# Order of one attention slot: scores and attention times v ahead of the second mixing, and the high copy between score copy and exponential

## Chip, cores and metric

The kernel runs on 1 core of one Trainium2 chip. The metric is the device time of one execution in microseconds (us), the median of several runs. Each run of the kernel before is listed below.

## What is computed

A talking-heads attention (4 batches, 12 heads, 448 tokens, 64 per head) is followed by two feed-forward blocks of 1792 tokens. The change lies in the attention alone. `w_pre` and `w_post` are 12 x 12 matrices that mix the heads before and after the softmax.

```python
scores = scale * np.matmul(q, k.transpose(0, 1, 3, 2))
scores = np.einsum('bhij,hg->bgij', scores, w_pre)      # first mixing
scores = scores - np.max(scores, axis=-1, keepdims=True)
attn = np.exp(scores)
attn = attn / (np.sum(attn, axis=-1, keepdims=True) + 1e-09)
attn = np.einsum('bhij,hg->bgij', attn, w_post)         # second mixing
return np.matmul(attn, v).astype(np.float32)            # a times v
...
a = x @ w1
b = x @ w2
h = a * b @ w3
x = h @ w_out
...
h = x @ w_in
r = np.maximum(h, 0.0)
return ((r * r) @ w_out).astype(np.float32)
```

## The kernel before

**Tiles.** The queries of each batch are cut into four groups of 110, 110, 110 and 118 rows, 16 groups `s` in all. For each group the scores of all 12 heads are made on TensorE in six pairs of heads (`qk`, L241, six matmuls each), copied from PSUM by ScalarE (`evict_s`, L248, the score copy) into one tile `S`. A DMA (`regroup`) then gathers 10 queries x 12 heads = 120 rows of 448 scores into a block `Bt`. There are 180 blocks `u`, 11 or 12 for each group. Everything that follows is done block by block:

- `premix` (L284, TensorE, float32, four matmul records for two blocks): the first mixing, into one of three PSUM banks `p`.
- `negmax` (L298, VectorE): the negative maximum of each row.
- `expo` (L306, ScalarE): the exponential with the row sum. It is the last reader of the bank `p`; its release comes with a second record, ACTIVATION_READ_ACCUMULATOR.
- `norm` (L322, L336, VectorE, for two blocks at once): the inverse of the sum.
- `split_h` (L353 on GpSimd, in some blocks L351 on ScalarE) and `split_l` (L367 on VectorE for even blocks, L364 and L365 on GpSimd for odd ones): the scaled exponential as two float16 halves `EH` and `EL`.
- `postmix` (L380, TensorE): the second mixing, 12 matmuls of 120 columns, into one of two PSUM banks `o`; the attention comes out transposed.
- `at_h` (L396, ScalarE): the high half of that result in float16, the high copy; `at_l` (L402, VectorE): the low half, which needs the high one and frees the bank `o`.
- `av` (L494, TensorE): attention times v for two heads of a whole group, in two parts of 12 matmuls each, once all blocks of the group have been through `at_l`. The result is copied by `put_xh` (L513, ScalarE) and `put_xl` (L522, VectorE) for every third pair of heads.

**Slots.** A loop over `u` from 0 (line 1332) writes the order of every engine's queue out by hand (`tc.manual_schedule()`, line 624), so the order in the program is the order on each engine. Slot `u` does the maximum and the exponential of block `u`, the halves of blocks `u-2` and `u-3`, `postmix(u-4)`, `at_h(u-5)` and `at_l(u-5)`. An odd slot does the first mixings of two blocks, `u+1` and `u+2`; an even slot none.

**Events.** Work for whole groups is put on slots ahead of the loop (lines 549 to 620): a list of `(kind, number, function, arguments)` for each slot, where `kind` is one of LOAD, FIRST, MID, LOW and END, and `do(kind)` carries out those of one kind. `qk` and `av` are END, with `store_x` and two steps of the scale of v; `evict_s` is FIRST of the next slot (MID in two crowded slots), `put_xh` FIRST and `put_xl` MID of the slot behind the third and sixth `av`. The splits of q, k and v are MID and LOW. Six slots of each group of 11 or 12 carry one `qk`, and most of these one `av` too.

**The order in a slot** is, in short: LOAD; `at_h`; two `premix` (odd slots); `negmax`; FIRST; `expo`; `norm`, `split_h`, `split_l`; `postmix`; `at_l`; MID; LOW; END; `regroup`. `AHEAD` is (5, 7): in these two slots `postmix` comes ahead of `premix`. `NB` is 180, `LAG` is 4 and `LEAD` is 5.

Of the kernel before, what the change touches and what calls it, by code (L numbers as in the profile page):

```python
# [24 lines left out]
LAG = 4  # L25
# [9 lines left out]
def talking_heads_attention_moe_moe2(  # L35
# [55 lines left out]
    def psum(pool, tag, dt=F32):  # L91
        return pool.tile([P, 512], dt, tag=tag, name=tag)
# [171 lines left out]
    NB = len(BLK)  # L264
# [16 lines left out]
    def premix(u):  # L281
        n = BLK[u][2]
        pt = psum(ps_p, "p")
        nc.tensor.matmul(  # L284
            pt[: n * H, :S],
            wpre_k.rearrange("p t g -> p (t g)")[: n * H, : n * H],
            Bt.pop(u)[: n * H],
            start=True,
            stop=True,
        )  # L290
        Pp[u] = pt

    def negmax(u):

        n, j = BLK[u][2] * H, u % 2
        if j == 0:
            nsum[u] = nsum[u + 1] = bp.tile([NBK, 6, 2], F32, tag="st", name="st", bufs=3)
        nc.vector.tensor_reduce(  # L298
            nsum[u][:n, 0, j : j + 1], Pp[u][:n, :S], axis=AX.X, op=ALU.max, negate=True
        )  # L300

    def expo(u):
        n, j = BLK[u][2] * H, u % 2
        t = nsum[u]
        e = bp.tile([NBK, EG, EW], F32, tag="E", name="E", bufs=4)[:, :, : S // EG]
        nc.scalar.activation(  # L306
            e[:n],
            Pp.pop(u)[:n, :S].rearrange("p (a b) -> p a b", a=EG),
            AF.Exp,
            bias=t[:n, 0, j : j + 1],  # L310
            scale=1.0,
            accum_out=t[:n, 1, j : j + 1],
        )
        Ex[u] = e

    def norm(u):

        t = nsum[u]
        rows = [BLK[x][2] * H for x in (u, u + 1)]
        if rows[0] == rows[1]:  # L320
            n = rows[0]
            nc.vector.tensor_scalar(  # L322
                t[:n, 2:5, :],
                t[:n, 1, :].unsqueeze(1).to_broadcast([n, 3, 2]),
                1e-9, 2.0 ** -11, op0=ALU.add, op1=ALU.mult,
            )
        else:
            for a in (0, 1):
                n = rows[a]
                nc.vector.tensor_scalar(  # L330
                    t[:n, 2, a : a + 1], t[:n, 1, a : a + 1], 1e-9, 2.0 ** -11,
                    op0=ALU.add, op1=ALU.mult,
                )
        for a in [slice(0, 2)] if rows[0] == rows[1] else [slice(0, 1), slice(1, 2)]:
            n = rows[a.start]
            nc.vector.reciprocal(t[:n, 5, a], t[:n, 2, a])  # L336
# [7 lines left out]
    def low_on_pool(u):  # L344
        return u % 2 == 1

    def split_h(u):
        n = BLK[u][2] * H
        EH[u] = bp.tile([NBK, S], F16, tag="EH", name="EH", bufs=4)
        if low_on_pool(u) and (u in full or u >= LAST_EH):  # L350
            nc.scalar.activation(seven(EH[u][:n]), Ex[u][:n], AF.Copy, scale=inverse(u))  # L351
            return
        nc.gpsimd.tensor_scalar(  # L353
            seven(EH[u][:n]), Ex[u][:n], inverse(u), 1.0, op0=ALU.mult, op1=ALU.mult
        )

    def split_l(u):
        n = BLK[u][2] * H
        e = Ex.pop(u)[:n]
        EL[u] = bp.tile([NBK, S], F16, tag="EL", name="EL", bufs=4)  # L360
        a, b = (seven(x[:n]) for x in (EL[u], EH[u]))
        if low_on_pool(u):
            f = bp.tile([NBK, EG, EW], F32, tag="F", name="F", bufs=1)[:n, :, : S // EG]
            nc.gpsimd.tensor_scalar(f, e, inverse(u), 1.0, op0=ALU.mult, op1=ALU.mult)  # L364
            nc.gpsimd.tensor_tensor(a, f, b, op=ALU.subtract)  # L365
        else:
            nc.vector.scalar_tensor_tensor(  # L367
                a, e, inverse(u), b, op0=ALU.mult, op1=ALU.subtract
            )

    def postmix(u):
        s, m, nr = BLK[u]
        n = nr * H
        pt = psum(ps_o, "o")
        hh, ll = EH.pop(u), EL.pop(u)
        wh = wpost_h[nr].rearrange("p g t -> p (g t)")
        wl = wpost_l[nr].rearrange("p g t -> p (g t)")
        for c in range(NCH):
            for i, (a, w) in enumerate(((hh, wh), (hh, wl), (ll, wh))):
                nc.tensor.matmul(  # L380
                    pt[:CP, c * n : (c + 1) * n],
                    a[:n, c * CP : (c + 1) * CP],
                    w[:n, :n],
                    start=(i == 0),
                    stop=(i == 2),
                )
        Po[u] = pt

    def at_h(u):
        s, m, nr = BLK[u]  # L390
        if m == 0:
            ATs[s] = tuple(
                bp.tile([CP, NCH, H, RMAX], F16, tag=f"AT{x}", name=f"AT{x}") for x in "hl"
            )
        src = Po[u][:CP, : NCH * nr * H].rearrange("p (c g t) -> p c g t", c=NCH, g=H)
        nc.scalar.copy(ATs[s][0][:, :, :, m * NR : m * NR + nr], src)  # L396

    def at_l(u):
        s, m, nr = BLK[u]
        src = Po.pop(u)[:CP, : NCH * nr * H].rearrange("p (c g t) -> p c g t", c=NCH, g=H)  # L400
        a = slice(m * NR, m * NR + nr)
        nc.vector.tensor_tensor(  # L402
            ATs[s][1][:, :, :, a], src, ATs[s][0][:, :, :, a], op=ALU.subtract
        )
# [127 lines left out]
    def load_x(z, b, i, k):  # L532
        if (b, i) == (0, 0):
            xall.append(sp.tile([P, NDC, NT], F16, tag="S", name="x"))
        n = S if b < B - 1 else sum(ROWS[:-2])
        cs = slice(i * NDC // k, (i + 1) * NDC // k)
        nc.sync.dma_start(xall[z][:, cs, b * S : b * S + n], x_d[z, b, :, cs, :n])
# [9 lines left out]
    LOAD, FIRST, MID, LOW, END = range(5)  # L547
# [85 lines left out]
    def keep_busy(n):  # L633
        for _ in range(n):
            nc.tensor.matmul(idle, zeros[:, :P], zeros, start=True, stop=True)
# [58 lines left out]
    AHEAD = (5, 7)  # L694
# [450 lines left out]
    def load_to(n):  # L1145
        while done[0] < min(n, limit[0]):
            load_w(done[0])
            done[0] += 1
# [180 lines left out]

    mlp_start = first[NSUP - 1] - 4  # L1330
    early = iter(())
    for u in range(NB + LAG + 2):
        if u == NB - LEAD:
            limit[0] = len(chunks)
            load_to(2 + LOADS)
        if u == mlp_start:
            kst.close()
            pools["w"] = ctx.enter_context(tc.tile_pool(name="wp", bufs=2, side="right"))
        if u in W_LOADS:
            load_to(W_LOADS.index(u) + 1)  # L1340
        if u == c0:
            early = (x for x in pair_steps(0, None) if x[2])
        if u == NB - LEAD + 1:
            for b in range(B):
                load_x(1, b, 0, 1)
        work = sorted(events.pop(u, []), key=lambda e: e[0])

        def do(now):
            for kind, _, f, a in work:
                if kind == now:  # L1350
                    f(*a)

        do(LOAD)
        if 0 <= u - LAG - 1 < NB - LAG:
            at_h(u - LAG - 1)
        if u in AHEAD:
            postmix(u - LAG)
        if u % 2:
            for x in (u + 1, u + 2):
                if x < NB:  # L1360
                    premix(x)
        if u in FILL:
            keep_busy(FILL[u])
        if u < NB:
            negmax(u)
        do(FIRST)
        if u < NB:
            expo(u)
        if u % 2 == 0 and 0 <= u - 2 < NB:
            norm(u - 2)  # L1370
        if 0 <= u - 2 < NB:
            split_h(u - 2)
            if low_on_pool(u - 2):
                split_l(u - 2)
        if 0 <= u - 3 < NB and not low_on_pool(u - 3):
            split_l(u - 3)
        if 0 <= u - LAG < NB and u not in AHEAD:
            postmix(u - LAG)
        if 0 <= u - LAG - 1 < NB - LAG:
            at_l(u - LAG - 1)  # L1380
        do(MID)
        do(LOW)
        for eng, cost, f in islice(early, STEPS.get(u, 0)):
            f()
        do(END)
        if NB <= u < NB + LAG:
            assert next(early, None) is None
            allow[0] = place["w1", 2]
            at_h(u - LAG)
            at_l(u - LAG)  # L1390
            first_tile(u - NB)
        if u + LEAD < NB:
            regroup(u + LEAD)
        if u - mlp_start in X_HIGH:
            load_x(0, *divmod(X_HIGH.index(u - mlp_start), 2), 2)
# [923 lines left out]
```

## Time and profile before

| | |
|---|---|
| runs of the kernel before | 1226.0, 1224.4, 1220.56 us (median 1224.4) |
| profiled execution | 1220.15 us, span of its trace 1218.4 us |
| TensorE matmuls busy | 1206.0 us (99% of the span) |
| TensorE weight loads | 746.8 us (61%) |
| VectorE (DVE) | 946.1 us (78%) |
| ScalarE (ACT) | 804.5 us (66%) |
| GpSimd (POOL) | 587.9 us (48%) |
| chain that ended last | TensorE 88%, VectorE 7%, ScalarE 2% |

The profile is one execution, read on the core's engines. PE is TensorE's matmuls, PEld its weight loads, DVE VectorE, ACT ScalarE, POOL GpSimd. Attention takes the first 440 us or so of the span. The matmul records overlap, since TensorE is a pipeline and the end of a matmul is modelled: a second mixing's matmuls are shown as 0.22 us each and start 0.05 us apart. So the busy share of TensorE says little about short stalls, and the starts say more. In the timeline consecutive instructions of one line and shape stand in one row with their count. A row ends with the idle time in front of it and what released it, where there was any.

### The profile page before, as it was taken

How to read it: one execution, taken by the hardware profiler on the slowest of the kernel's cores; microseconds unless marked ns; L12 is line 12 of the kernel's file. 1: busy time of each engine (PE TensorE's matmuls, PEld its weight loads, DVE VectorE, ACT ScalarE, POOL GpSimd, SP SyncE). 2: the span in 40 equal slices, each digit the busy share in tenths (PEclk: the TensorE clock that was granted, in tenths of full speed). 3: DMA queues.
4: the chain of work that ended last, by engine and by line, in shares of the span. 5: the costliest groups of instructions: out<-in, count | busy, mean ns of one | idle time of the engine just before them, and what ended most of it. 6: DMA issues, size and time to landing. Idle time of an engine off the chain costs nothing.

```text
span 1218.4 us, 26225 instructions
## 1 busy us (share of the span) xinstructions
PE 1206.0 (99%) x9904; PEld 746.8 (61%) x9904; DVE 946.1 (78%) x1690; ACT 804.5 (66%) x1620; POOL 587.9 (48%) x569
## 2 busy tenths in 40 slices
PE   7999999999999999999999999999999999999998
PEld 4666777676676765555558975555555555666665
DVE  6988899888889956766676875798778775999773
ACT  6888888878888735554454555568879776654430
POOL 4898788889879610101001311446143424666340
PEclk9999999999999999999999999999999999999999
DMA  6466555655645853655533537354478659656562
GB/s 196 128 160 166 136 146 135 170 126 152 177 115 163 240 131 101 161 135 158 138 131 127 190 120 245 110 168 167 162 259 280 236 192 325 196 159 184 175 193 79
DMA packets 139907, 205.02 MB, mean 168 GB/s; under 512 B 33828, under 2 KB 114852, under 8 KB 139780
## 3 DMA queue, kind: packets, MB, share of 16 engines
q1 hardware_dynamic: 139220, 202.41, 56.3%
q8 instruction: 78, 1.28, 0.5%
q0 software_dynamic: 560, 0.93, 0.4%
q14 instruction: 49, 0.40, 0.1%
HBM read 114.60 MB, written 50.16 MB: 135 GB/s over the span
## 4 chain that ended last, share of the span: by engine, by line
PE 88%; DVE 7%; ACT 2%; DMA 1%; issue 1%; SPq 0%; POOL 0%; ACTq 0%; DVEq 0%; POOLq 0%
PE mm L1259 25%; PE mm L1873 16%; PE mm L2125 16%; PE p L284 8%; PE o L380 7%; PE mm L1537 5%; PE s L241 4%; PE a L494 4%; DVE ATl L402 2%; DVE st L298 2%; DVE EL L367 2%; PE p L1259 1%; ACT E L306 1%; ACT ATh L396 0%; DMA Bt<-S 0%
## 5 line engine op out<-in xcount | busy, mean ns | idle before, releaser
L1259 PE MATMUL mm<-x,w 128*128 128x448 f16 x1044 | 197.7, 352 | 0.0
L1259 PEld LDWEIGHTS <-w 128*128 128x128 f16 x1134 | 110.5, 98 | 102.8
L1873 PE MATMUL mm<-x,wq 128*128 128x448 f16 x882 | 169.3, 352 | 0.0
L284 PE MATMUL p<-Bt,wpre_k 120*120 120x448 f32 x360 | 159.2, 560 | 3.1 <-DMA Bt<-S 2.6
L2125 PEld LDWEIGHTS <-ao 128*128 128x128 f16 x1176 | 115.0, 98 | 76.0
L380 PEld LDWEIGHTS <-EH 120*112 120x112 f16 (+1 forms) x1440 | 124.6, 130 | 44.7 <-issue 36.5
L1873 PEld LDWEIGHTS <-wq 128*128 128x128 f16 x882 | 86.0, 98 | 79.8 <-issue 0.3
L402 DVE TENSOR_TENSOR ATl<-o,ATh 112x480 f16<-112x480 f32 x180 | 116.1, 645 | 24.2 <-ACT ATh L396 23.7
L353 POOL TENSOR_SCALAR EH<-E,st 120x448 f16<-120x448 f32 (+1 forms) x152 | 112.6, 749 | 46.0 <-DVE st L336 34.6
L306 ACT ACTIVATE E<-p,st 120x448 f32<-120x448 f32 x180 | 116.3, 646 | 23.9 <-DVE st L298 14.6
L396 ACT CAST ATh<-o 112x480 f16<-112x480 f32 x180 | 101.1, 562 | 39.8 <-PE o L380 34.8
L380 PE MATMUL o<-wph,EH 120*112 120x120 f16 x720 | 124.0, 219 | 1.4 <-DVE ATl L402 1.1
L380 PE MATMUL o<-wph,EL 120*112 120x120 f16 x720 | 122.0, 216 | 0.0
L380 PE MATMUL o<-wpl,EH 120*112 120x120 f16 x720 | 122.0, 216 | 0.0
L365 POOL TENSOR_TENSOR EL<-F,EH 120x448 f16<-120x448 f32 (+1 forms) x90 | 104.0, 1155 | 31.7 <-issue 18.5
L298 DVE TENSOR_REDUCE st<-p 120x1 f32<-120x448 f32 x180 | 110.2, 613 | 1.2 <-PE p L284 0.7
L1259 PE MATMUL mm<-h,M 128*128 128x448 f16 x576 | 110.2, 353 | 0.0
L2125 PE MATMUL mm<-x,ao 128*128 128x384 f16 x588 | 96.5, 326 | 0.0
L2125 PE MATMUL mm<-ow,ao 128*128 128x384 f16 x588 | 96.0, 326 | 0.0
L380 PEld LDWEIGHTS <-EL 120*112 120x112 f16 x720 | 93.6, 130 | 0.0
L367 DVE SCALAR_TENSOR_TENSOR EL<-E,st,EH 120x448 f16<-120x448 f32 (+1 forms) x90 | 82.9, 921 | 11.1 <-POOL EH L353 10.6
L1259 PEld LDWEIGHTS <-M 128*128 128x128 f16 x576 | 55.9, 98 | 52.0 <-DVE M L1447 0.8
(266 smaller groups left out, 2535.8 us busy)
## 6 DMA issues: line engine op xcount, KB each, us to landing
Bt<-S SPq DMA_DIRECT2D x176, 210.0 KB
raw<-in_moe_w_out_dram SPq DMA_DIRECT2D x24, 768.0 KB
g<-ev SPq DMA_DIRECT2D x64, 224.0 KB
gt<-g SPq DMA_DIRECT2D x56, 256.0 KB
raw<-in_moe_w_in_dram SPq DMA_DIRECT2D x16, 768.0 KB
raw<-in_moe_w_dram SPq DMA_DIRECT2D x14, 768.0 KB
raw<-in_moe_w_dram SPq DMA_DIRECT2D x16, 512.0 KB
kept_out<-xa SPq DMA_DIRECT2D x16, 384.0 KB
```

Source lines behind the costliest of these rows:

```text
L284: nc.tensor.matmul(pt[: n * H, :S], wpre_k.rearrange("p t g -> p (t g)")[: n * H, : n * H], Bt.pop(u)[: n * H], start=True, stop=True,)
L298: nc.vector.tensor_reduce(nsum[u][:n, 0, j : j + 1], Pp[u][:n, :S], axis=AX.X, op=ALU.max, negate=True)
L306: nc.scalar.activation(e[:n], Pp.pop(u)[:n, :S].rearrange("p (a b) -> p a b", a=EG), AF.Exp, bias=t[:n, 0, j : j + 1], scale=1.0, accum_ou ...
L353: nc.gpsimd.tensor_scalar(seven(EH[u][:n]), Ex[u][:n], inverse(u), 1.0, op0=ALU.mult, op1=ALU.mult)
L365: nc.gpsimd.tensor_tensor(a, f, b, op=ALU.subtract)
L367: nc.vector.scalar_tensor_tensor(a, e, inverse(u), b, op0=ALU.mult, op1=ALU.subtract)
L380: nc.tensor.matmul(pt[:CP, c * n : (c + 1) * n], a[:n, c * CP : (c + 1) * CP], w[:n, :n], start=(i == 0), stop=(i == 2),)
L396: nc.scalar.copy(ATs[s][0][:, :, :, m * NR : m * NR + nr], src)
L402: nc.vector.tensor_tensor(ATs[s][1][:, :, :, a], src, ATs[s][0][:, :, :, a], op=ALU.subtract)
L1259: nc.tensor.matmul(pt[:, :S], w[a][:, cs], x[z][:, sl], start=(c == 0 and i == 0), stop=(c == len(parts) - 1 and i == 2),)
L1873: nc.tensor.matmul(pt[:, :S], w[:, a, c * P : (c + 1) * P], xop(t, b, kb, c), start=(start and c == 0 and m == 0), stop=(c == 2 and m == 2 ...
L2125: nc.tensor.matmul(pt[:, :OH], y[:, a, q * P : (q + 1) * P], ow[g, q][kb][:, w], start=(start and q == 0 and m == 0), stop=(q == NQ - 1 an ...
```

## The change

The loop of the slots is edited in five places. A slot behind number 7 that carries a `qk` or an `av` is called a `visit`. In a visit `postmix(u-4)` is issued behind END, so behind the scores and a times v of the slot, instead of ahead of `at_l`. In the slot behind a visit (`behind`) `at_h(u-5)` is issued behind FIRST, so behind the score copy and `put_xh`, and ahead of `expo(u)`; before, it was the first of the slot. Nothing is computed differently, and no instruction is added or removed.

```diff
@@ -1329,6 +1329,7 @@
     early = iter(())
+    behind = False
     for u in range(NB + LAG + 2):
@@ -1351,7 +1352,8 @@
         do(LOAD)
-        if 0 <= u - LAG - 1 < NB - LAG:
+        visit = max(AHEAD) < u < NB and any(e[0] == END and e[2] in (qk, av) for e in work)
+        if 0 <= u - LAG - 1 < NB - LAG and not behind:
             at_h(u - LAG - 1)
@@ -1364,6 +1366,8 @@
         do(FIRST)
+        if behind:
+            at_h(u - LAG - 1)
         if u < NB:
             expo(u)
@@ -1374,7 +1378,7 @@
-        if 0 <= u - LAG < NB and u not in AHEAD:
+        if 0 <= u - LAG < NB and u not in AHEAD and not visit:
             postmix(u - LAG)
@@ -1383,6 +1387,9 @@
         do(END)
+        if visit:
+            postmix(u - LAG)
+        behind = visit and u + 1 < NB
         if NB <= u < NB + LAG:
```

## Rows read from the trace of the kernel before

**Rows 1.** Windows: busy us and count by engine, 40 to 395 us, then clock, DMA
```profile
40.00:395.00 355.00, 353.89 (x4577) 247.41 (x4576) 310.09 (x670) 295.56 (x656) 302.66 (x333) 1.00 0.57 148
```

**Rows 2.** Waits of weight loads, same stretch: total us, times, longest us
```profile
PEld p L284 <- ACT E L306: 13.3, 35, 0.8
```

**Rows 3.** Timeline of TensorE, beat of slots 45 and 46: start, us, what
```profile
116.62 1.76 PE L284 MATMUL p<-Bt,wpre_k 120*120 120x448 f32 x4
...
118.22 0.22 PE L380 MATMUL o<-wph,EH 120*112 120x120 f16 x1
...
121.06 1.39 PE L284 MATMUL p<-Bt,wpre_k 120*120 120x448 f32 x3
```

**Rows 4.** Timeline of TensorE, beat of slots 91 and 92
```profile
222.12 1.72 PE L284 MATMUL p<-Bt,wpre_k 120*120 120x448 f32 x4
222.92 0.54 PE L284 MATMUL p<-Bt,wpre_k 120*120 120x448 f32 x1
223.67 0.22 PE L380 MATMUL o<-wph,EH 120*112 120x120 f16 x1
...
224.25 0.22 PE L380 MATMUL o<-wph,EL 120*112 120x120 f16 x1
224.40 0.46 PE L241 MATMUL s<-kh,qh 64*110 64x448 f32 x2
224.69 0.36 PE L241 MATMUL s<-kl,qh 64*110 64x448 f32 x2
224.89 0.37 PE L241 MATMUL s<-kh,ql 64*110 64x448 f32 x2
225.19 0.24 PE L494 MATMUL a<-ATh,Vh 112*64 112x110 f16 x2
...
225.90 0.26 PE L380 MATMUL o<-wph,EH 120*112 120x120 f16 x1
...
226.52 0.22 PE L380 MATMUL o<-wph,EL 120*112 120x120 f16 x1
226.57 1.34 PE L284 MATMUL p<-Bt,wpre_k 120*120 120x448 f32 x3
```

**Rows 5.** Timeline of TensorE: second mixings of even event slots behind a stall
```profile
49.79 0.21 PE L380 MATMUL o<-wph,EH 120*112 120x120 f16 x1
...
184.08 0.21 PE L380 MATMUL o<-wph,EH 120*112 120x120 f16 x1 [0.47 <-DVE ATl L402]
...
383.43 0.21 PE L380 MATMUL o<-wph,EH 120*112 120x120 f16 x1 [0.36 <-DVE ATl L402]
```

**Rows 6.** Timeline of ScalarE, the beat of rows 4
```profile
222.32 0.56 ACT L396 CAST ATh<-o 112x480 f16<-112x480 f32 x1
222.78 0.64 ACT L306 ACTIVATE E<-p,st 120x448 f32<-120x448 f32 x1
...
224.50 0.57 ACT L396 CAST ATh<-o 112x480 f16<-112x480 f32 x1 [0.39 <-PE o L380]
225.30 0.91 ACT L248 COPY S<-s 110x896 f32<-110x896 f32 x1 [0.23 <-PE s L241]
226.10 0.64 ACT L306 ACTIVATE E<-p,st 120x448 f32<-120x448 f32 x1
226.63 0.20 ACT L306 ACTIVATION_READ_ACCUMULATOR E<-p,st 120x1 f32 x1
```

**Rows 7.** Timeline: first mixings of odd beats that waited for an exponential
```profile
92.24 1.94 PE L284 MATMUL p<-Bt,wpre_k 120*120 120x448 f32 x4
...
101.38 2.03 PE L284 MATMUL p<-Bt,wpre_k 120*120 120x448 f32 x4
102.12 0.21 ACT L306 ACTIVATION_READ_ACCUMULATOR E<-p,st 120x1 f32 x1
102.39 0.64 PE L284 MATMUL p<-Bt,wpre_k 120*120 120x448 f32 x1
...
365.29 1.98 PE L284 MATMUL p<-Bt,wpre_k 120*120 120x448 f32 x4
```

## Prediction, made before the changed kernel was run

> **What bounds the kernel now.** I read the busy table of the attention stretch first, since the change touches nothing behind it [rows 1]. From 40 to 395 us TensorE is busy for 353.89 of 355 us; VectorE, ScalarE and GpSimd have 13 to 17% free, and the granted clock is 1.00. So TensorE's work sets the pace, and another order of its instructions can win only what TensorE waits, or the turn-round between kinds of matmul. Next I read the waits of TensorE's weight loads [rows 2]: 13.3 us in 35 places for the exponential (L306), which frees the bank that a first mixing (L284) writes. Much of that is a loader waiting beside a running matmul; so I then read the timeline from start to start, where a true stall shows as a longer step.
>
> Two slots make one beat: two first mixings (L284), two second mixings (L380), and in nearly every beat one set of scores (L241) and a times v (av, L494). The 94 slots that the change treats ("event slots", counted from lines 549 to 620) are 44 even and 50 odd ones. In a beat whose event slot is even, TensorE's order is first, first, second, second, scores, av [rows 3]; where it is odd: first, first, second, scores, av, second [rows 4]. Both beats take the same time: 121.06 - 116.62 = 4.44 us and 226.57 - 222.12 = 4.45 us.
>
> **Direct work on TensorE.** Nothing is added or removed; 12 matmuls of a second mixing move behind the scores and av.
> - Even beats become first, first, second, scores, av, second: the order of today's odd beat. Step by step: the first mixings take 118.22 - 116.62 = 1.60 us behind av [rows 3] and 223.67 - 222.12 = 1.55 us behind a second mixing; in exchange the second mixing that comes behind av lengthens from 224.25 - 223.67 = 0.58 to 226.52 - 225.90 = 0.62 us [rows 4]. Sum: 0.0, as the two beat lengths say.
> - Odd beats become first, first, scores, av, second, second. One neighbour is new: scores straight behind a first mixing. Bounds from the turns of today: from a first to a second mixing nothing is lost (from the later first mixing at 222.92 to 223.67 are 0.75 us, two passes of 0.38); from a second mixing into the scores 224.40 - 224.25 = 0.15, where matmuls of a mixing stand 0.05 apart, so 0.10 is lost; from scores into av 225.19 - 224.89 = 0.30 against 224.89 - 224.69 = 0.20 inside the scores, 0.10 again [rows 4]. So the old turn's 0.10 goes and the new one costs 0 to 0.10: a gain of 0 to 0.10 a beat, 0 to 5 us over 50. I take 0: the two turns that lose time are those where the tile shape changes (120x112, 64x110, 112x64), behind a step of 0.05 and one of 0.20 alike, and the new turn changes it too. The Trainium skill (TensorEngine Tiling (Array Packing), Key Properties) says that a change of tiling mode drains TensorE; the two turns agree, and no row shows the new one. By that rule this part is 0 us, without it -5 us.
>
> **Stalls that go.** In an even beat the later second mixing stands 0.58 us behind the earlier one, and it takes the bank of the one two before it, which the low part (L402) must have read. In five places it stalls, read as the step less 0.05: 0.24 (at 49.79, the first), 0.63, 0.16, 0.04 and 0.52 us (at 383.43, the last), 1.6 us in all; the two large ones show as idle time even by the modelled ends [rows 5]. All five are in even event slots, where this mixing now starts later by scores and av, 225.90 - 224.25 = 1.65 us [rows 4], more than any stall. Gain: 1.6 us. Next late behind the bank would be the half EL, and it wins the same 1.65 us.
>
> **What comes later.** ScalarE's high copy (L396) needs the second mixing; in odd beats that now ends later. And the change puts the copy behind the score copy (L248, 0.91 us) and, every third event, the copy of av's result (L513). Queued behind the high copy on ScalarE is the exponential of the same slot; behind that waits the second first-mixing of the next beat, for its bank (there are three). Today, in the beat of [rows 4, 6]: high copy 224.50, score copy 225.30, exponential 226.10 to 226.83. The mixing that waits is due 222.92 - 222.12 = 0.80 us into the next beat, at 226.57 + 0.80 = 227.37: 0.54 us of slack.
>
> After: the scores start 0.63 us earlier (0.58 and a step of 0.05), so the score copy starts at 225.30 - 0.63 = 224.67 and hands over 0.80 later (226.10 - 225.30), at 225.47. The moved mixing issues its last matmul at 226.52 - 0.58 - 0.05 = 225.89; high copy 0.25 later (224.50 - 224.25), at 226.14. So the copy placed in front costs nothing here: the wait for the second mixing hides it, with 0.67 us to spare (some 0.3 with L513); without that cover it would cost its 0.80. Exponential 0.46 after the copy (222.78 - 222.32), at 226.60; released after 0.73 (226.83 - 226.10), at 227.33; the mixing goes 0.06 after a release (102.39 - 102.33 [rows 7]), at 227.39. It is due at 227.37: a tie.
>
> So the slack of 0.54 is used up in odd beats: 4.45 us by TensorE's work, 4.47 by the loop through second mixing, high copy, exponential, first mixing, scores and av. What a lost race costs is seen where it is lost today: the two mixings at 101.38 last 2.03 us against 1.72 [rows 4, 7], +0.31, of which 0.10 is a weight load that wasn't done ahead (0.64 against 0.54). There are six such places, the first at 92.24 and the last at 365.29, of 0.18 to 0.31 us, 1.5 us in all; I count half as gone, since the score copy in front of the exponential no longer waits behind the high copy there. Of the 50 odd event slots 9 have another one right behind, whose scores and av give the loop over 1.6 us more; 41 remain. Bounds for each: 0 (in time) and 0.2 (tie lost by 0.1, 0.1 of weight load). I take 0.05, near the computed 0.02: 2.0 us. In about ten of them ScalarE has more to do (L433, L351 or L466 beside L513), so that its copy is late by itself: 0.1 more each, 1.0 us.
>
> On VectorE the low part (L402) waits for the high copy, and behind it are queued the splits, the next maximum (L298) and EL. VectorE has 44.9 of 355 us free [rows 1], 0.56 us a beat, and the maximum behind the low part is wanted by ScalarE only after one more high copy. Cost 0; where splits fill the gap, up to 0.3 a beat. In even beats the exponential comes no later, for the same two copies were ahead of it before. SP's DMA issues and GpSimd's work keep their order; nothing is moved past them. The last 35 us of attention have shorter beats and more av: +-0.5.
>
> **Sum.** -1.6 - 0.7 + 2.0 + 1.0 = +0.7 us. The profiled execution took 1220.15 us (span 1218.4), 4.25 below the median of 1224.4, at the lower end of the three runs (1220.56 to 1226.0). So 1221 for a profile like that one, and 1225.0 for the median.
>
> **The rivals.**
> - The tie is lost everywhere (slower). In odd beats the loop through the exponential takes TensorE's place as the bound. Place: the second first-mixing of each beat; it decides at a release later than 0.06 us before the mixing is due. Price: 41 x 0.2 = 8.2, less 1.6: 1231. For it: the slack computes to -0.02, and ScalarE has extra work in some beats. Against it: today's six losses add up to 1.5 us only. Chance 0.13.
> - The new turn is free (faster): scores behind a first mixing load their weights under its 0.38 us pass. 50 x 0.10 + 1.6 = 6.6: 1218. Against it: the turn behind the scores' 0.20 us pass hides nothing [rows 4]. Chance 0.06.
> - That the order isn't what the change says is no rival: the kernel writes it out by hand.
>
> **How the numbers follow.** Forecast 1225.0, chance 0.81, with its bounds (from -1.6 - 1.5 to about +6) 1221 to 1231. With the scatter of a median and the faster rival's end the range is 1218 to 1232. A measurement of this kernel can tell about 0.5%, 6.1 us: faster than 1218.3 has 0.06, slower than 1230.5 has 0.13, the rest 0.81.
>
> **What would show it.** Right: beats of 4.44 to 4.50 us of either kind; no stall on L402 at a second mixing of an even event slot; ScalarE's wait for the high copy's mixing now behind the score copy; first mixings of up to 1.9 us in odd beats. Wrong: odd beats of 4.35 (the free turn), or of 4.6 and above with the wait for L306 far over 13.3 us (the lost tie). A low part that starts long after its high copy, with splits queued ahead of it, would break the step on VectorE.

## The result, and the profile after

The changed kernel takes 1238.82 us (median of 4 runs, 1237.25 to 1239.52) where the kernel before took 1223.71 beside it (1220.56 to 1226.0): a ratio of 1.0127, 95% interval 1.0109 to 1.0145. It is slower by about 15 us. The forecast was 1225.0 with a range up to 1232; no case named in it reaches this far. The profiled execution took 1239.29 us (span 1237.6), at a granted clock of 1.00 as before, so the clock is no cause. Lines up to L1331 have the same numbers in both kernels.

The busy windows of [rows 1], from 40 to 395 us, of the kernel after (length, then busy us and count of TensorE, its weight loads, VectorE, ScalarE, GpSimd, then clock, DMA share, GB/s):

```profile
40.00:395.00 355.00, 345.47 (x4384) 228.78 (x4382) 293.99 (x645) 282.34 (x631) 283.21 (x318) 1.00 0.55 143
```

TensorE had 1.1 us without work in this stretch, now 9.5, and every engine got less done. The last second mixing starts at 456.55 us instead of 439.25. So TensorE no longer sets the pace everywhere; the question is who keeps it waiting. The waits of VectorE, ScalarE and TensorE, 40 to 450 us (us in total, times, longest), of the kernel before:

```profile
DVE ATl L402 <- ACT ATh L396: 23.6, 34, 1.5
DVE xt L522 <- ACT xt L513: 9.6, 15, 0.9
ACT E L306 <- DVE st L298: 11.7, 22, 1.3
PE p L284 <- ACT E L306: 0.2, 1, 0.2
```

and, VectorE first, of the kernel after:

```profile
DVE ATl L402 <- ACT ATh L396: 59.4, 79, 2.4
```

The low part (L402) now waits 36 us more for its high copy (L396), in 79 places instead of 34, and the wait for the copy of av's result, L513, has gone. It has not been cured: L522 stands behind L402 in VectorE's queue, and when its turn comes L513 has long been done. The waits of weight loads (PEld), TensorE and ScalarE in the same stretch, after:

```profile
PEld p L284 <- ACT E L306: 29.8, 43, 2.0
PE p L284 <- ACT E L306: 4.3, 9, 1.2
PE a L494 <- DVE Vl L473: 2.9, 6, 0.9
PE a L494 <- DVE xt L522: 1.3, 2, 1.1
ACT E L306 <- DVE st L298: 28.4, 39, 1.5
ACT E L306 <- DVE st L322: 16.3, 19, 1.9
```

ScalarE's two waits, both for VectorE, were 11.7 and 6.6 us before, the first line 15.6 (13.3 in the shorter stretch of [rows 2]); av's waits for VectorE (L494) are new, and TensorE's own wait for an exponential was 0.2 us in one place. All eight places in which av stands lie in even beats, and all nine in which a first mixing stands for an exponential lie in odd beats or in beats with two event slots. There are two different losses: a small one in clean odd beats, and one that comes from VectorE's queue and reaches TensorE through av in even beats and through the exponential in odd ones. A beat of each kind follows.

**A clean odd beat** (slots 91 and 92 again, to set beside [rows 4] and [rows 6]; start, us, engine, line), TensorE after:

```profile
230.99 1.82 PE L284 MATMUL p<-Bt,wpre_k 120*120 120x448 f32 x4
232.74 0.45 PE L241 MATMUL s<-kh,qh 64*110 64x448 f32 x2
...
235.54 1.82 PE L284 MATMUL p<-Bt,wpre_k 120*120 120x448 f32 x4
```

and ScalarE after:

```profile
235.11 0.56 ACT L396 CAST ATh<-o 112x480 f16<-112x480 f32 x1 [0.56 <-PE o L380]
235.57 0.64 ACT L306 ACTIVATE E<-p,st 120x448 f32<-120x448 f32 x1
236.09 0.20 ACT L306 ACTIVATION_READ_ACCUMULATOR E<-p,st 120x1 f32 x1
```

The next beat starts at 235.54: the beat lasts 4.55 us, 0.10 more than the 4.45 of [rows 4], and the four first mixings 1.82 instead of 1.72. The exponential is released at 236.09 + 0.20 = 236.29, the waiting mixing can go 0.06 later, at 236.35, and by today's turns is due at 235.54 + 0.80 = 236.34. The tie of the prediction is there to 0.01 us, and it is lost.

**A loaded even beat**, from 168.88 to 174.36 us (5.48), ScalarE, VectorE and TensorE after:

```profile
169.12 0.89 ACT L248 COPY S<-s 118x896 f32<-118x896 f32 x1
169.91 0.46 ACT L513 ACTIVATE xt<-a 128x330 f16<-128x330 f32 x1
170.24 0.57 ACT L396 CAST ATh<-o 112x480 f16<-112x480 f32 x1
...
170.84 0.66 DVE L402 TENSOR_TENSOR ATl<-o,ATh 112x480 f16<-112x480 f32 x1 [0.59 <-ACT ATh L396]
171.42 0.49 DVE L522 SCALAR_TENSOR_TENSOR xt<-a,xt 128x330 f16<-128x330 f32 x1
171.83 1.20 DVE L473 SCALAR_TENSOR_TENSOR Vl<-vraw,vs,Vh 112x512 f16<-112x512 f32 x1
172.03 0.22 PE L494 MATMUL a<-ATl,Vh 112*64 112x110 f16 x2
...
172.95 0.61 DVE L298 TENSOR_REDUCE st<-p 120x1 f32<-120x448 f32 x1
173.08 0.24 PE L494 MATMUL a<-ATh,Vl 112*64 112x110 f16 x2 [0.83 <-DVE Vl L473]
...
173.68 0.63 ACT L306 ACTIVATE E<-p,st 120x448 f32<-120x448 f32 x1 [1.78 <-DVE st L322]
```

and the same beat (slots 65 and 66) before, from 163.40 to 167.85 us (4.46 by the unrounded starts):

```profile
163.03 0.55 ACT L396 CAST ATh<-o 112x480 f16<-112x480 f32 x1
163.48 0.91 ACT L248 COPY S<-s 118x896 f32<-118x896 f32 x1
...
164.09 0.65 DVE L402 TENSOR_TENSOR ATl<-o,ATh 112x480 f16<-112x480 f32 x1
...
165.19 0.74 DVE L473 SCALAR_TENSOR_TENSOR Vl<-vraw,vs,Vh 112x512 f16<-112x512 f32 x1
165.84 0.62 DVE L298 TENSOR_REDUCE st<-p 120x1 f32<-120x448 f32 x1
...
166.58 0.64 ACT L306 ACTIVATE E<-p,st 120x448 f32<-120x448 f32 x1 [0.19 <-DVE st L322]
```

Before, the high copy stood ahead of the score copy, and VectorE was through with low part, L522, half of v (L473) and maximum (L298) 166.46 - 163.40 = 3.06 us into the beat. After, score copy and L513 stand ahead of the high copy; the low part waits for it at the head of VectorE's queue; L522 and L473 wait behind the low part, and the maximum is done only 4.68 us into the beat. av needs both a free bank (L522) and the half of v (L473). That it waits for L522 costs next to nothing here: from scores to av 0.31 us pass, against 0.30 in [rows 4]. The wait for L473 costs 173.08 - 172.03 = 1.05 us where matmuls of av stand 0.05 apart. The exponential stands 1.78 us for VectorE. This beat costs 1.02 us more.

**A loaded odd beat**, from 157.11 us (slots 61 and 62), after; the chain begins in the beat ahead of it:

```profile
152.68 0.66 DVE L402 TENSOR_TENSOR ATl<-o,ATh 112x480 f16<-112x480 f32 x1 [1.59 <-ACT ATh L396]
154.26 0.62 DVE L298 TENSOR_REDUCE st<-p 120x1 f32<-120x448 f32 x1
154.91 0.63 ACT L306 ACTIVATE E<-p,st 120x448 f32<-120x448 f32 x1 [1.18 <-DVE st L298]
...
158.53 1.01 PE L284 MATMUL p<-Bt,wpre_k 120*120 120x448 f32 x2 [0.46 <-ACT E L306]
```

The low part waits 1.59 us, the maximum, queued behind it and behind other work of its slot, comes late, ScalarE waits 1.18 us for it and from then on has work without a gap up to the next exponential (157.73 to 158.48), for which the first mixing stands 0.46 us. This beat costs 0.72 us more, and 0.11 in the run e3_low_last below.

**Where the 15 us lie.** I measured every beat from the start of its first mixings to the next ones, in each kernel's profile, and took the difference to the kernel before (us; one profile each; the slots ahead of 9, whose order is unchanged, differ by up to 2.1 between these profiles, and the tail's last beats scatter by as much; the first row adds up to 16.1, where the medians differ by 15.1). "Odd" and "even" are the 37 and 34 beats with one event slot, "double" six beats with two, "tail" the last seven:

| kernel | odd | even | double | tail |
|---|---|---|---|---|
| after | +7.91 | +4.50 | +1.63 | +2.09 |
| e1_even | +0.18 | +3.87 | +2.67 | -0.14 |
| e2_odd | +6.59 | +0.26 | +0.62 | +3.05 |
| e3_low_last | +2.82 | +0.97 | +0.88 | +0.75 |
| e4_exp_first | +19.74 | +5.13 | +5.16 | +3.83 |
| e5_both | +2.81 | +1.15 | +2.52 | +3.34 |
| e12_xl_first | +5.56 | +3.43 | +1.49 | +0.70 |

Of the 7.91 us in odd beats, 17 clean beats with +0.08 to +0.14 each make 1.70; ten heavy ones with +0.3 to +1.7 make 7.0. Of the 4.50 in even beats, seven heavy ones with +0.4 to +1.1 make 5.2, and two gain 0.61 and 0.52. The clean beats and the heavy ones of both kinds are followed through the runs below.

### The profile page after: what moved, and what is told of

It reads as the page before. It is cut to its first block, busy times and chain, and to the rows that moved or that the text cites. A ratio compares the mean times of both kernels' runs of the same rounds, so it can differ in the third digit from the quotient of the medians.

```text
span 1237.6 us, 26211 instructions
## 1 busy us (share of the span) xinstructions
PE 1213.3 (98%) x9904; PEld 736.9 (60%) x9904; DVE 941.5 (76%) x1690; ACT 803.1 (65%) x1620; POOL 581.7 (47%) x569
## 4 chain that ended last, share of the span: by engine, by line
PE 74%; DVE 11%; ACT 6%; DMA 4%; issue 3%; POOL 0%; SPq 0%; DVEq 0%; ACTq 0%; POOLq 0%
PE mm L1259 16%; PE mm L2132 15%; PE mm L1880 15%; PE p L284 7%; PE o L380 6%; PE mm L1544 5%; PE s L241 3%; PE a L494 3%; DMA Bt<-S 2%; DVE ATl L402 2%; DVE st L298 2%; ACT E L306 1%; PE p L1259 1%; DVE Vl L473 1%; ACT ATh L396 1%
## 5 line engine op out<-in xcount | busy, mean ns | idle before, releaser
L284 PE MATMUL p<-Bt,wpre_k 120*120 120x448 f32 x360 | 162.2, 564 | 10.6 <-DMA Bt<-S 5.5
L402 DVE TENSOR_TENSOR ATl<-o,ATh 112x480 f16<-112x480 f32 x180 | 116.6, 648 | 61.7 <-ACT ATh L396 61.5
L380 PEld LDWEIGHTS <-EH 120*112 120x112 f16 (+1 forms) x1440 | 120.1, 130 | 25.8 <-issue 16.6
L396 ACT CAST ATh<-o 112x480 f16<-112x480 f32 x180 | 101.5, 565 | 30.7 <-PE o L380 30.0
L365 POOL TENSOR_TENSOR EL<-F,EH 120x448 f16<-120x448 f32 (+1 forms) x90 | 101.5, 1128 | 36.6 <-issue 23.2
L298 DVE TENSOR_REDUCE st<-p 120x1 f32<-120x448 f32 x180 | 110.0, 612 | 1.8 <-PE p L284 1.8
L284 PEld LDWEIGHTS p<-Bt,wpre_k 120*120 120x120 f32 x360 | 55.0, 182 | 58.1 <-ACT E L306 31.7
```

The source lines that it names most:

```text
L284: nc.tensor.matmul(pt[: n * H, :S], wpre_k.rearrange("p t g -> p (t g)")[: n * H, : n * H], Bt.pop(u)[: n * H], start=True, stop=True,)
L298: nc.vector.tensor_reduce(nsum[u][:n, 0, j : j + 1], Pp[u][:n, :S], axis=AX.X, op=ALU.max, negate=True)
L380: nc.tensor.matmul(pt[:CP, c * n : (c + 1) * n], a[:n, c * CP : (c + 1) * CP], w[:n, :n], start=(i == 0), stop=(i == 2),)
L402: nc.vector.tensor_tensor(ATs[s][1][:, :, :, a], src, ATs[s][0][:, :, :, a], op=ALU.subtract)
```

## The experiments

Two theories. **L**, the loop: second mixing, high copy, exponential, first mixing, scores, av is now as long as TensorE's own work, and the first mixing that waits for the bank loses time in every odd beat. **Q**, the queue: VectorE's low part waits for a later high copy, and L522, L473 and the next maximum wait behind it; loss where a beat has that work. All edits are against the kernel after, unless the kernel before is named.

**Half the change each.** e1_even treats only even event slots, e2_odd only odd ones:

```diff
-        visit = max(AHEAD) < u < NB and any(e[0] == END and e[2] in (qk, av) for e in work)
+        visit = max(AHEAD) < u < NB and any(e[0] == END and e[2] in (qk, av) for e in work) and u % 2 == 0
```

(e2_odd: `u % 2 == 1`.)

> The change in even event slots only; odd ones keep the order of before. Against before, the changed kernel lost 4.5 us in beats with an even event slot, 7.9 us in beats with an odd one, 1.6 us where both are event slots, 2.1 us in the tail. Theory L (the loop through the exponential and the bank of the first mixing) is at work in odd slots only: it expects the kernel of before less its five stalls, 1222 us. Theory Q (VectorE's low part L402 waits for the later high copy, and the halves of v, the copy of av's result and the next maximum queued behind it come late) expects the loss of the even beats to stay, +4 to +5: 1228 us.

> The change in odd event slots only. Theories L and Q both expect the loss of the odd beats, of the double ones and most of the tail, +10 us: 1233 to 1235 us. If this and the run with even slots alone add up to the whole loss of 15 us, the two kinds of beat don't disturb each other.

e1_even: 1228.73 us against 1222.83, ratio 1.0053 (1.0038 to 1.0068). e2_odd: 1230.95, 1.0074 (1.0058 to 1.009). 5.9 + 8.1 = 14.0 us: the two halves add up. e1_even came out as Q had it, e2_odd 2 us below what both gave. The even half, in which five stalls go, loses nearly three quarters of what the odd one does; so the loop through odd beats, L, is not the whole. How much of the odd half is L's, this pair can't tell.

**The low part last.** e3_low_last keeps the whole change, but behind an event slot VectorE does the splits and L522 ahead of the low part, as ScalarE does L513 ahead of the high copy:

```diff
-        if 0 <= u - LAG - 1 < NB - LAG:
+        if 0 <= u - LAG - 1 < NB - LAG and not behind:
             at_l(u - LAG - 1)
         do(MID)
         do(LOW)
+        if behind:
+            at_l(u - LAG - 1)
```

> The whole change, but in a slot behind an event slot the low part (L402) is issued behind the splits of the slot (MID and LOW) and not ahead of them. Theory Q expects av's waits for L473 and L522 to go and with them nearly all but the lost weight load of 0.1 us in some 35 odd beats: 1226 to 1229 us. Theory L expects the odd beats to stay as slow as with the change: 1233 to 1236 us.

1227.43 us against 1222.83, ratio 1.0044 (1.0026 to 1.0061). By the ratios 1.0127 - 1.0044 = 0.83%, about 10 of the 15 us, come back, from an edit on VectorE alone. The waits of e3_low_last, 40 to 450 us:

```profile
DVE ATl L402 <- ACT ATh L396: 28.5, 48, 1.5
ACT E L306 <- DVE st L298: 16.4, 38, 1.2
PEld p L284 <- ACT E L306: 27.7, 46, 2.0
PE p L284 <- ACT E L306: 1.7, 2, 1.2
PE o L380 <- DVE ATl L402: 1.2, 2, 1.0
PE a L494 <- DVE ATl L402: 0.7, 1, 0.7
```

VectorE's wait and ScalarE's wait for the maximum are nearly back at the level of before; the loader's wait for the exponential (L) is not. Beat by beat the two theories come apart: the ten heavy odd beats fall from +7.0 to +1.2 us, the seven heavy even ones from +5.2 to +0.4, and the 17 clean odd beats stay at +1.7. So Q is shown, in both kinds of beat: 10.6 us of these profiles come back, 1.4 of them in one beat that also waits for a DMA (see the end). L remains, with other losses that are told at the end. The last two lines are the price: in one even beat a second mixing (1.0 us) and in another av (0.7 us) now waits for the low part, which comes last.

**Only L522 ahead of the low part**, whole change (e12_xl_first):

```diff
+        if behind:
+            for kind, _, f, x in work:
+                if f is put_xl:
+                    f(*x)
+            work = [e for e in work if e[2] is not put_xl]
         if 0 <= u - LAG - 1 < NB - LAG:
             at_l(u - LAG - 1)
```

> The whole change, with one repair on VectorE: in a slot behind an event slot the low copy of av's result (L522, every third event) goes ahead of the low part of the second mixing (L402), as its high copy (L513) now goes ahead of L396 on ScalarE. The other splits stay behind. Theory Q has two readings. If the harm is that VectorE's order no longer follows ScalarE's (L522 ready, but queued behind L402), most of the 11 us that the repair with all splits gave comes back: 1226 to 1230 us. If the harm is that the halves of v and the other splits, which wait for nothing on ScalarE, stand behind L402, little comes back: 1233 to 1236 us.

1234.6 us against 1225.04, ratio 1.0082 (1.0054 to 1.0109). The waits of e12_xl_first, 40 to 450 us:

```profile
DVE ATl L402 <- ACT ATh L396: 41.4, 60, 1.6
PE a L494 <- DVE Vl L473: 2.4, 6, 0.9
```

av's waits for L522 are all but gone, those for L473 are still there, and VectorE's wait lies between 59.4 and 28.5. By the ratios L522 behind the low part is worth 0.45% (5.5 us), the splits behind it another 0.38% (4.6 us); that each costs something is shown, how much is not: the intervals of the three kernels all but touch. The time lies where the second reading had it, 1233 to 1236 us.

**The same edit in the kernel before** (e11_low_alone): mixings and high copy stay where they were, only the low part goes last.

> Only the low part goes behind the splits, in slots behind an event slot; second mixing and high copy stay. It says what this repair costs or gives by itself. Theory Q: in the kernel of before VectorE waits 24 us for the high copy and TensorE loses next to nothing by it, so 0 +-2 us: 1221 to 1224 us.

1231.7 us, ratio 1.0087 (1.0072 to 1.0102); expected were 1221 to 1224. The same move that gives 10 us back in the changed kernel costs 10 in the old one. The waits, 40 to 450 us:

```profile
DVE xt L522 <- ACT xt L513: 24.1, 21, 2.6
PE o L380 <- DVE ATl L402: 8.6, 17, 1.3
```

In the old order ScalarE does the high copy first and L513 behind it; now VectorE waits at L522 for L513 (24.1 us instead of 9.6) while the low part, whose input is there, stands behind, and second mixings wait for it (8.6 us, 1.1 before). A low part that comes last is not better in itself: what costs is that VectorE's order is not ScalarE's. The beats say the same: the 26 beats with an L522 sum to +6.1 us, and the 26 that have none, neither in them nor in the beat ahead, to +0.4.

**Only the high copy moved** (e8_high_only), the second mixing where it was before; and the same with the low part last (e9_high_low). Against the kernel before, `visit` and `behind` as in the change:

```diff
-        if 0 <= u - LAG - 1 < NB - LAG:
+        if 0 <= u - LAG - 1 < NB - LAG and not behind:
             at_h(u - LAG - 1)
@@
+        if behind:
+            at_h(u - LAG - 1)
         if u < NB:
             expo(u)
```

> The second mixing stays where it was, only the high copy goes behind the score copy and the copy of av's result. Theory L: the exponential has the same work in front of it as before and its release does not move, 0 us: 1223. Theory Q: the high copy is 0.8 to 1.1 us later in some 90 slots and holds VectorE's low part and the splits behind it: 1226 to 1230 us.

> The second mixing stays where it was; the high copy goes behind the score copy (which alone cost 17 us) and the low part behind the splits. Theory Q: the loss of the high copy alone came about because the low part, waiting for it, held VectorE's queue; with the splits in front the loss falls to 0 to 5 us: 1222 to 1227 us. If the loss were the late release of the second mixing's bank or of av's input, the low part would be later still and the time stays at 1236 us or more.

e8_high_only: 1238.79 us, ratio 1.0139 (1.0124 to 1.0154): as much as the whole change, which neither theory expected. e9_high_low: 1234.45 against 1221.51, 1.011 (1.0094 to 1.0125), expected were 1222 to 1227. Waits, 40 to 450 us, of e8_high_only:

```profile
ACT S L248 <- PE s L241: 19.8, 36, 1.9
PE o L380 <- DVE ATl L402: 7.5, 14, 1.0
```

and of e9_high_low:

```profile
ACT S L248 <- PE s L241: 34.4, 55, 1.9
PE o L380 <- DVE ATl L402: 6.6, 13, 1.5
```

With the second mixing early and its copy late, ScalarE waits at the score copy for the scores while the high copy, whose input is done, stands behind (19.8 and 34.4 us, 6.6 before), and the late low part holds up a second mixing (7.5 and 6.6 us, 1.1 before). So the late high copy alone suffices for a loss of this size, but by other waits; that the totals are equal doesn't show that the mixing's move is free. The two parts of the change belong together: with copy and low part late, the mixing's move wins (1.011 with it early, e9_high_low, 1.0044 with it late, e3_low_last). In e9_high_low VectorE's order is ScalarE's again and 1.1% are still lost; its waits point to ScalarE's order, which is no longer TensorE's.

**Only the second mixing moved** (e7_high_early), the high copy at the head of the slot as before:

```diff
-        if 0 <= u - LAG - 1 < NB - LAG and not behind:
+        if 0 <= u - LAG - 1 < NB - LAG:
             at_h(u - LAG - 1)
@@
-        if behind:
-            at_h(u - LAG - 1)
```

> The second mixing is moved as in the change, the high copy stays first of its slot, ahead of the score copy. Theory L: in odd beats the score copy (0.80 us on ScalarE) then stands between the late high copy and the exponential, so each of 41 odd beats pays 0.8 us more than the tie: 1250 to 1257 us. Theory Q: the high copy is no later than with the change, so VectorE waits no more than there, 1235 to 1240 us.

1269.25 us, ratio 1.039 (1.0375 to 1.0406): more than the 1250 to 1257 of L, and far above Q's 1235 to 1240. ScalarE of e7_high_early in a clean odd beat, behind the high copy, which waits 1.69 us for the second mixing:

```profile
249.60 0.91 ACT L248 COPY S<-s 110x896 f32<-110x896 f32 x1
250.39 0.65 ACT L306 ACTIVATE E<-p,st 120x448 f32<-120x448 f32 x1
```

and the mixings that wait for exponentials, the one of the beat before and the one behind these lines, on TensorE:

```profile
245.82 1.01 PE L284 MATMUL p<-Bt,wpre_k 120*120 120x448 f32 x2 [0.65 <-ACT E L306]
...
251.18 1.01 PE L284 MATMUL p<-Bt,wpre_k 120*120 120x448 f32 x2 [0.65 <-ACT E L306]
```

From one such mixing to the next 251.18 - 245.82 = 5.36 us pass, 0.91 more than the 4.45 of before: the score copy's 250.39 - 249.60 = 0.79 in the loop, and 0.10 of a weight load that isn't done ahead. This is the price that the prediction put on the copy without the cover of the second mixing ("its 0.80"), and it shows the loop: TensorE waits for the exponential, as L says. Single odd beats sum to +30.5 us and the six double beats, which the 41 of the estimate leave out, to +13.2.

**The exponential ahead of the high copy**, to take the copy out of the loop, in even slots behind an event slot (e4_exp_first); and with the low part last (e5_both):

```diff
-        if behind:
+        if behind and u % 2:
             at_h(u - LAG - 1)
         if u < NB:
             expo(u)
+        if behind and u % 2 == 0:
+            at_h(u - LAG - 1)
```

> The whole change, but in even slots behind an event slot the exponential goes ahead of the high copy, so the bank of the first mixing is released without a wait for the second mixing. Theory L expects the weight-load waits for L306 to fall to the 13 us of before, odd beats of 4.45 us and 1227 to 1230 us. Theory Q expects the 0.1 us of some 35 clean odd beats back and no more: 1235 us.

> The whole change with both repairs: the low part (L402) behind the splits, and in even slots behind an event slot the exponential ahead of the high copy. The low part behind the splits alone left 4.6 us of the 15. Theory L says these are the first mixing's lost races in odd beats, and that the exponential in front takes them back: 1222 to 1225 us. Theory Q says that the high copy, another 0.62 us later, makes VectorE and the bank of the second mixing late again, as in the run with the exponential first alone (L402 kept a second mixing waiting 21 times there): 1230 us or more.

e4_exp_first: 1256.57 us, ratio 1.0281 (1.0265 to 1.0296), far outside what either theory gave. e5_both: 1233.43 against 1221.61, 1.0095 (1.008 to 1.011), also above what was expected. A wait of e4_exp_first, 40 to 450 us:

```profile
PE o L380 <- DVE ATl L402: 10.7, 21, 1.2
```

The high copy comes still later, so VectorE waits longer for it (74.7 us), and the low part now comes too late for the second mixing's bank in 21 places: another loop through the same two engines. In e5_both, TensorE in the stretch of clean odd beats:

```profile
222.42 1.72 PE L284 MATMUL p<-Bt,wpre_k 120*120 120x448 f32 x4
226.86 1.72 PE L284 MATMUL p<-Bt,wpre_k 120*120 120x448 f32 x4
```

226.86 - 222.42 = 4.44: with the exponential 0.46 us earlier the 0.10 is gone and the first mixings are back at 1.72. That shows L's part, and that it is small: the 17 clean odd beats sum to +0.3 us instead of +1.7, and more is lost elsewhere (e5_both is 0.51% slower than e3_low_last).

**Halves with the low part last**, e6_even_low and e10_odd_low (the edits of e1_even or e2_odd and of e3_low_last together):

> The change in even event slots only, and the low part (L402) behind the splits in the slots behind them. Even slots alone cost 5.9 us. Theory Q: all of that was VectorE's queue, so it goes, and the stalls of even slots stay away: 1221 to 1224 us. Theory L has no part in even slots and says the same as before, 1222; if 4 us or more remain, both theories lack something in even beats.

> The change in odd event slots only, with the low part behind the splits in the slots behind them. Odd slots alone cost 8.1 us. Theory L: what is left is the lost weight load of 0.09 to 0.10 us in some 30 clean odd beats, +3 us, 1225 us. Without theory L, 1222 us; were odd beats slow for a reason of their own, 1228 us or more.

e6_even_low: 1225.33 us, ratio 1.0032 (1.0022 to 1.0042). e10_odd_low: 1226.48, 1.0039 (1.0025 to 1.0053). The first is above Q's 1221 to 1224, the second 1.5 us above L's 1225. Both ratios stay above 1, though the large stalls of the even slots are gone in e6_even_low: single even beats still sum to +0.79 us (a stall behind the late low part in each of two beats, +0.66 and +1.0, eats what the five stalls gave), double beats to +2.37 and the tail to +2.95 (in a profile that is 2.6 us above this run's median). In five of the six double beats scores that come right behind the scores of the slot before wait for their score copy, 2.0 us in all. No version of the change beats the kernel before.

## Why the prediction was wrong, step by step

- **Direct work on TensorE, 0: right.** In the clean odd beat after, the last first mixing starts at 230.99 + 1.82 - 0.54 = 232.27 and the scores at 232.74: 0.47, a pass of 0.38 and 0.09 lost. The new turn costs what the old ones did, and the rival of the free turn (1218) is out. The Trainium skill's rule that a change of tiling mode drains the engine (TensorEngine Tiling (Array Packing), Key Properties) agrees with this 0.09. No run tells a drain from a weight load that isn't done ahead.
- **Stalls that go, -1.6: the mechanism right.** The two beats with the large stalls are 0.61 and 0.52 us shorter in the kernel after. In the same kind of beat 4.50 us net are lost.
- **Lost races of today, -0.7: right in four places of six.** The odd beats at 92.24, 101.38, 300.25 and 309.33 us of the kernel before are shorter by 0.61 us together; the other two are longer.
- **The tie: computed right, mis-sized.** Slack and loop came out to 0.01 us. But 0.05 a beat, "near the computed 0.02", isn't a possible outcome: a mixing whose bank comes free at the last moment has no weight load ahead of it, and that load's 0.10 then lies in the loop itself, so each next beat loses it again. Clean odd beats lost 0.10 each. The first pass of the later first mixing is stretched in this way (0.64 us instead of 0.54) in 6 places before and in 37 after. 31 more at 0.10 are about 3 us. That this equals the 2.0 + 1.0 of the sum is luck, since it is another price in another number of places; this term did not make the miss. The rival "tie lost everywhere" (0.2 each) had the right mechanism at twice its price, and it doesn't reach 1239 either.
- **"So the copy placed in front costs nothing here": true of the beat it was worked out in only.** There the second mixing is the later input (0.56 us of wait in the fence above). In the loaded even beat the high copy shows no wait at 170.24: it stands behind the score copy and L513, and nothing hides them. e8_high_only and e7_high_early bracket the step: the copy late alone costs the whole 1.4%, the copy early behind a late mixing costs 3.9%.
- **"On VectorE ... Cost 0; where splits fill the gap, up to 0.3 a beat": the step that failed.** The prediction named what is queued behind the low part and then followed only the maximum, in a beat without events. It didn't follow L522, which frees av's bank, nor L473, which av reads: the consumer of both is TensorE, within the same beat. And of the maximum it said that ScalarE wants it "only after one more high copy", so that the exponential in even beats "comes no later": ScalarE's wait for it (L298) rose from 11.7 to 28.4 us, and TensorE's for the exponential from 0.2 to 4.3. The 0.56 us free in a beat were an average over 355 us; in the beats in question VectorE is loaded, and its wait (0.59 us in the even beat above, 1.59 ahead of the odd one) is on the path to av or to the exponential. And it looked for the sign in the wrong place: for splits ahead of the low part, where the trouble is splits behind it (putting them ahead is the cure). e3_low_last prices the step, which the sum had at nothing: 0.83%, about 10 us, by the intervals 7 to 13.
- **The tail, +-0.5:** +2.09, in one profile; +0.75 with the low part last.

**What stays open.** e3_low_last is still 0.44% (5.4 us) slower, and late first mixings are stretched in 37 places there too: some 3 us of it. The rest is spread over double beats (+0.88), the tail (+0.75) and the two new stalls behind the late low part (+0.66 and +1.02); no run takes these apart. One odd beat of the kernel after loses 1.70 us at a wait for a DMA into the block `Bt` (0.27 in e3_low_last); whether it is the change's can't be told from one profile.

## What to carry to other kernels

Engines that work in order and hand over to each other should keep their queues in the same order: whoever moves an instruction on one should move its consumer, and what stands between old and new place, on the next. Here that gave back 10 of 15 us; the same move without its partner cost as much (e11_low_alone), and two engines in step were not enough where the third was not (e9_high_low). Follow every instruction behind a wait to its own consumer, in the fullest slot and not in the typical one; an engine's free share is an average and covered nothing in the fullest beats here. A slack that computes to zero is better counted as lost, at the full price of what can no longer be done ahead.

## What the runs showed of the hardware

- A float32 first mixing whose bank comes free just in time starts at the right moment and still costs 0.10 us, in each of 17 clean odd beats (1.82 against 1.72 for four); releasing the bank 0.46 us earlier takes it away (e5_both, 4.44 against 4.55; +0.3 us over the 17 instead of +1.7).
- The turn from a float32 mixing (120x120) to the scores (64x110) loses 0.09 us, although the pass ahead of it lasts 0.38, as long as the one behind which a second mixing starts without loss [rows 4].
